# Attention on two double PSUM banks and feed-forward on four banks from step 8; shared blocks added into the PSUM bank in the last four chunks

## The chip, the core and the metric

The kernel runs on one core of a Trainium2 chip. Five engines work side by side, each through its own queue in program order: TensorE (PE) multiplies matrices and writes only PSUM; VectorE (DVE) and ScalarE (ACT) do elementwise work and read and write PSUM and SBUF; GpSimd (POOL) works on SBUF; SyncE (SP) issues most of the DMAs. They meet through semaphores. PSUM has eight banks; a bank holds 512 float32 numbers in each of 128 partitions. The metric is device time in microseconds; lower is better.

## The reference, cut to what matters

```
# attention, B,H,S,D = 4,8,768,48, per head and per time t
k_n = k / (|k| + 1e-6)
y[t] = q[t] @ state
state = state + beta[t] * outer(k_n[t], v[t] - state^T k_n[t])
# y goes to x of shape (B*S, H*D) = (3072, 384), then the feed-forward
h = x @ w_in                                        # w_in: 384 x 2048
g = maximum(h, 0) + alpha * minimum(h, 0)           # alpha: one slope per column of h
out = g @ w_out                                     # w_out: 2048 x 384
```

A recurrence over 768 positions, then a feed-forward of 3072 tokens with a PReLU between two matrix products. All is float32.

## The kernel before, in words

**Attention.** The 768 positions are cut into 12 chunks of 64. A chunk of all four batches is done in two *steps* (two batches each), so there are 24 steps n, and step n carries on the state of step n − 2. In each step the recurrence is solved with small matmuls: k times the state (`through_state`, L798), a triangular solve (`solve`, L823), the outputs (`outputs`, L836), the new state (`next_state`, L852), the query times the state (`query`, L783), grams of k for a step that comes nine later (`grams`, L500), small inverses (`between`, L732), and transposes of y into the feed-forward's input `xt` (`to_ffn`, L875). DVE inverts 32x32 blocks for four steps at a time (`eliminate`, L592 and L598). From step 8 on q, and from step 16 on k, are fetched as 32x32 blocks and turned by DVE (`turn_q`, L465; `turn_k`, L477). After its turn, every second `turn_k` has SP fetch the next chunk's keys; `load_q(n + 3)` fetches q for a later step.

**Feed-forward.** A chunk is 256 tokens. Chunks 2 to 7: `ffn_in` (L965) goes through eight *pairs* of 128 columns of h, each pair into one PSUM bank taken from `ps_ffn()`; ACT then writes Relu(−h) to SBUF (L975) and DVE makes g from it and from h in PSUM, one instruction for each half (the *slope*, L977). `ffn_out_fast` (L1030) multiplies by w_out with a scheme of seven instead of eight block products, each into a bank from `ps_ffn()`; DVE adds them up (L1050) and forms sums of operands ahead of them (L919). Chunks 8 to 11: `ffn_in_fast` uses the seven-product scheme for the input as well. A pair has six sub-steps. Two are for the *shared* products (L1198), which go into a bank of their own, from which ACT copies them to SBUF (`z`, L1217) and POOL adds them up (L1222). Four are for the pair's *own* products (L1188, L1193), in bank i mod 3. Then DVE adds z to the own bank and writes the sum h to SBUF (L1227, `total`), ACT takes Relu of it into another SBUF tile (L1232, `below`), and DVE makes g (L1236, `slope`). `ffn_out_faster` (L1282) is their output, L1278 its adds. A small list, `Due`, says after how many sub-steps (PER = 6 to a pair) each of the three is put into the program.

**PSUM.** Two banks, `ffn_banks[0:2]`, always belong to the feed-forward. `banks(pair, single)` shares out the other six: `big` is a rotating list of double banks (tiles `p_pair`) for attention, and further single banks (tiles `p_more`) are appended to `ffn_banks`. At first there are three doubles and no single; with step LATE = 16 there are two doubles and two singles. `ps_ffn()` flips between banks 0 and 1 in both cases; the two further banks are used only by chunks 8 to 11.

**The order of the work.** The order on each engine is the order in which the program puts the instructions, and that is written by hand. Each step n of the main loop has three bursts of attention, each followed by a *stretch* of feed-forward pieces from the generator `tail`: `burst_a(n)` (outputs and new state of step n − 1, k times the state, and the query while n < LATE), a stretch; `turn_round(n)` (transposes of step n − 1), a stretch; `burst_b(n)` (solve, grams, small inverses, and for n + 1 ≥ LATE the query of step n + 1), a stretch. `stretch` weaves its feed-forward pieces with a share of the block inversion and with the pieces that the burst returned as `later`; these are spread evenly from the fraction `soon` of the stretch on (0.5 unless given). A stretch has 8 to 18 pieces; `ffn_in` advances one matmul call at a time, an output product two. A matmul call appears in the profile as two records.

The turns are in `later` of `burst_a`, `load_q` is called straight from `turn_round`. The diff touches `ps_ffn` (L101), `through_state` (L801), `pair` in `ffn_in_fast` (L1172 to L1243), `burst_a` (L1383 to L1394), `burst_b` (L1403), `turn_round` (L1421 to L1423) and the main loop (from L1855 on).

Of the kernel before, what the change touches and what calls it, by code (L numbers as in the profile page):

```python
# [25 lines left out]
FP32 = mybir.dt.float32  # L26
# [6 lines left out]
C = 64  # L33
# [2 lines left out]
BUSY = 8  # L36
EARLY = 8
FIRST = 6
LATE = 16
FAST_IN = 8  # L40

# [2 lines left out]
def kernel(  # L44
# [53 lines left out]
    turn = [0]  # L98

    def ps_ffn():  # L100
        turn[0] ^= 1  # L101
        return ffn_banks[turn[0]]

    def half(i):
# [684 lines left out]
    def through_state(n, p=None, p_y=None):  # L789
        if n >= N:  # L790
            return []
        c, bp = steps[n]
        if c == 0:
            rhs_[n] = by_parity(nv[n])
            return []
        p = region(p, G * (D + C), g=G)
        for g, a, t in quarters():
            nc.tensor.matmul(  # L798
                p[half(t ^ a), a, g], k_t[n][dims(a), g, half(t)], beside[bp][dims(a), t, g]
            )  # L800
        asked = query(n, p_y) if n < LATE else []  # L801

        r = work.tile([128, 2, G, D], FP32, name="r")
        v_in = by_parity(nv[n])
        rhs_[n] = r

        def less(to, own, a):
            nc.vector.tensor_tensor(  # L808
                out=r[to, a], in0=v_in[to, a], in1=p[own, a, :, 0:D], op=ALU.subtract
            )  # L810

        return [
            lambda: less(slice(0, 128), slice(0, 128), 0),
            lambda: less(half(0), half(1), 1),
            lambda: less(half(1), half(0), 1),
            *asked,
            lambda: masked(n, p[:, :, :, D : D + C]),
        ]
# [333 lines left out]
    def ffn_in_fast(c):  # L1152
# [19 lines left out]
        def pair(i):  # L1172
            p = ffn_banks[i % 3]
            q = quarter(ffn_banks[2 if i == 0 else 3])
            z, g = terms(i), act_of(c, i)
            if "less" not in held:
                held["less"] = work.tile([128, G, 128], FP32, name="k_t", bufs=EARLY + 1)
            r = held["less"] if i % 2 == 0 else quarter(held["block"][:, 512:1024])
            r = r.rearrange("p (f u) e -> p f (u e)", f=2)

            def w(k, f):
                return w_in[:, k, (2 * i + f) * 128 : (2 * i + f + 1) * 128]
# [40 lines left out]
                yield  # L1223

            def total():
                h = g.rearrange("p f i -> p (f i)")
                nc.vector.tensor_tensor(  # L1227
                    out=h, in0=p, in1=z.rearrange("p i e -> p (i e)"), op=ALU.add
                )

            def below():
                nc.scalar.activation(r, g, ACT.Relu, scale=-1.0)  # L1232

            def slope():
                for f in range(2):
                    nc.vector.scalar_tensor_tensor(  # L1236
                        out=g[:, f], in0=r[:, f], scalar=al_t[:, 2 * i + f : 2 * i + f + 1],
                        in1=g[:, f], op0=ALU.mult, op1=ALU.add,
                    )

            due.put(PER * (i + 1) + {0: PER, FP - 1: 2}.get(i, 3), total)
            due.put(PER * (i + 2) + {FP - 2: 1, FP - 1: -4}.get(i, 2), below)
            due.put(PER * (i + 2) + {FP - 2: 1, FP - 1: -2}.get(i, 5), slope)  # L1243
            for gen in (own(), common()) if i == 0 else (common(), own()):
                for _ in gen:
                    due.step()
# [126 lines left out]
    def burst_a(n):  # L1373

        soon, later = [], []
        b = ps_big()
        if n > JOINED:
            soon += outputs(n - 1, b[:, :, 0:WY])
            soon += next_state(n - 1, b[:, :, WY : 2 * WY])
            later.append(lambda: load_late(n + 1))  # L1380
        if n < N:
            p = ps_big()
            y = ps_big()[:, :, 0:WY] if n < LATE else None  # L1383
            soon += through_state(n, p[:, :, 0 : G * (D + C)], y)
            if n < JOINED + 2:
                soon += between_1(n + 1, b[:, :, 2 * WY : 2 * WY + G * HB])
            if n == JOINED:
                soon += grams(n + EARLY, big[-1][:, :, WY : WY + G * C])
                later.append(lambda: squares(n + EARLY + 1))
            later.append(lambda: load_v(n + 3))  # L1390
            if TURNED_K <= n + EARLY + 1 < N:
                later.append(lambda: turn_k(n + EARLY + 1))
            if n + 2 < N:
                later.append(lambda: turn_q(n + 2))  # L1394
        now(soon)
        return later

    def burst_b(n):
# [1 line left out]
        b, x = ps_big(), ps_big()  # L1400
        soon = solve(n, b[:, :, 0:WY])
        gram = grams(n + EARLY + 1, x[:, :, 0 : G * C])
        asked = query(n + 1, x[:, :, 0:WY]) if n + 1 >= LATE else []  # L1403
        wanted = [(n + 1, True, b[:, :, WY : WY + G * HB])]
        if n > JOINED:
            wanted.append((n + 2, False, b[:, :, 2 * WY : 2 * WY + G * HB]))
# [7 lines left out]
    def turn_round(n):  # L1414

        if n > JOINED:
            to_ffn(n - 1)
        if n == JOINED:
            flips(n + EARLY + 1, N)
            load_keys(steps[TURNED_K][0])  # L1420
        later = weigh(n + EARLY + 1)  # L1421
        load_q(n + 3)
        return later  # L1423

    def each(pieces):
        for x in pieces:
# [426 lines left out]
    FILLS = [(12, 10, 12), (12, 18, 12)]  # L1853
    put_off = []
    for n in range(JOINED, N):  # L1855
        if n == LATE:
            banks(2, 2)
        fill, share = FILL.get(n, FILLS[n % 2]), PIECES_OF.get(n, TURNS[n % NJ])
        extra = [[], [], []]
# [10 lines left out]
        later = turn_round(n)  # L1870
        if n == JOINED:
            extra[1].append((placing(n + 1, (1, 2, 3)), PLACING))
        stretch(fill[1], blocks, share[1], later, *extra[1])
        m, ends = (n + 6) // NJ, n % NJ == 2
        if ends and n > JOINED:
            for _ in blocks:
# [55 lines left out]
```

## Time and profile before

| | us |
|---|---|
| median of three runs | 656.41 |
| range of the three | 654.98 to 656.82 |
| profiled execution, its own time | 656.53 |
| span of its trace | 654.8 |
| PE busy | 633.8 |
| DVE busy | 504.4 |
| ACT busy | 254.3 |
| POOL busy | 94.5 |

The span runs from the first to the last instruction; 1.7 us of the execution's time lie outside it. A row of the timeline gives start, duration, engine, line, operation, output and inputs, shape and how many were merged; a bracket at its end gives the idle time of the engine before it and what ended it. A row of groups gives, behind the bar, busy us and mean ns of one, then the idle time ahead of them and its releasers. A row of waits gives total us, how often, and the longest. PE's granted clock was 0.997 of full speed over the span.

### The profile page before, as it was taken

How to read it: one execution, taken by the hardware profiler on the slowest of the kernel's cores; microseconds unless marked ns; L12 is line 12 of the kernel's file. 1: busy time of each engine (PE TensorE's matmuls, PEld its weight loads, DVE VectorE, ACT ScalarE, POOL GpSimd, SP SyncE). 2: the span in 40 equal slices, each digit the busy share in tenths (PEclk: the TensorE clock that was granted, in tenths of full speed). 3: DMA queues.
4: the chain of work that ended last, by engine and by line, in shares of the span. 5: the costliest groups of instructions: out<-in, count | busy, mean ns of one | idle time of the engine just before them, and what ended most of it. 6: DMA issues, size and time to landing. Idle time of an engine off the chain costs nothing.

```text
span 654.8 us, 21590 instructions
## 1 busy us (share of the span) xinstructions
PE 633.8 (97%) x9199; PEld 558.2 (85%) x9199; DVE 504.4 (77%) x1206; ACT 254.3 (39%) x599; POOL 94.5 (14%) x204
## 2 busy tenths in 40 slices
PE   6989999999998998999998999999999999999997
PEld 4678888666777987988987988988989999999997
DVE  4976998967999789759969768868969659468383
ACT  5977565345443342243242242232135145042140
POOL 6001211010000000000000000000035044062260
PEclk9989999999999999999999999999999999999999
DMA  7956735212252241242242122122122210100000
GB/s 121 295 131 160 228 74 144 62 37 48 46 87 35 48 76 27 42 68 41 42 73 35 26 40 38 26 42 35 26 45 32 45 32 3 35 5 2 26 0 25
DMA packets 145968, 39.26 MB, mean 60 GB/s; under 512 B 139040, under 2 KB 142256, under 8 KB 145872
## 3 DMA queue, kind: packets, MB, share of 16 engines
q1 hardware_dynamic: 144000, 37.40, 28.0%
q8 instruction: 72, 1.18, 0.7%
q10 hardware_dynamic: 1872, 0.49, 0.4%
q14 instruction: 24, 0.20, 0.1%
HBM read 33.14 MB, written 4.72 MB: 58 GB/s over the span
## 4 chain that ended last, share of the span: by engine, by line
PE 76%; DVE 14%; ACT 3%; DMA 2%; issue 2%; SPq 1%; POOL 1%; DVEq 0%; POOLq 0%; ACTq 0%
PE p_ffn L1030 17%; PE p_ffn L965 13%; PE p_more L1282 8%; PE p_ffn L1008 5%; PE p_more L1198 5%; PE p_ffn L1188 3%; PE p_ffn L1282 3%; PE p_ffn L1193 2%; DVE act L977 2%; PE p_pair L732 2%; PE p_pair L823 2%; DVE block L598 2%; PE p_pair L1435 2%; DVE prod L592 2%; PE p_pair L677 2%
## 5 line engine op out<-in xcount | busy, mean ns | idle before, releaser
L965 PE MATMUL p_ffn<-xt,w_in 128*128 128x256 f32 x768 | 178.2, 385 | 7.8 <-DVE act L977 7.7
L965 PEld LDWEIGHTS p_ffn<-xt,w_in 128*128 128x128 f32 x768 | 142.9, 191 | 29.9 <-ACT act L975 5.0
L975 ACT ACTIVATE act<-p_ffn 128x512 f32<-128x512 f32 x56 | 33.3, 595 | 97.4 <-PE p_ffn L965 97.3
L977 DVE SCALAR_TENSOR_TENSOR act<-act,al_t,p_ffn 128x256 f32<-128x256 f32 x112 | 48.3, 472 | 25.7 <-ACT act L975 25.7
L598 DVE TENSOR_TENSOR block<-block,prod 128x30 f32<-128x30 f32 (+9 forms) x150 | 49.9, 332 | 5.2
L1222 POOL TENSOR_TENSOR k_t<-k_t 128x128 f32<-128x128 f32 (+1 forms) x48 | 29.4, 612 | 166.6 <-ACT k_t L1217 164.1
L1030 PE MATMUL p_ffn<-w_out,act 128*128 128x192 f32 x288 | 49.6, 329 | 0.7 <-ACT act L975 0.7
L592 DVE TENSOR_TENSOR prod<-block 128x30 f32<-128x30 f32 (+9 forms) x150 | 48.6, 324 | 1.5
L1030 PEld LDWEIGHTS p_ffn<-w_out,act 128*128 128x128 f32 x288 | 46.5, 190 | 1.3 <-ACT act L975 1.0
L417 POOL TENSOR_TENSOR beta_t<-beta_t,rec 128x8 f32<-128x8 f32 x24 | 6.2, 257 | 286.3 <-DVE rec L411 268.1
L877 ACT COPY xt<-p_pair 128x384 f32<-128x384 f32 x22 | 10.4, 478 | 92.3 <-PE p_pair L875 78.5
L1222 POOL TENSOR_TENSOR block<-block 128x128 f32<-128x128 f32 (+1 forms) x48 | 27.6, 576 | 16.0 <-ACT block L1217 13.5
L1188 PE MATMUL p_ffn<-xt,w_in 128*128 128x256 f32 x96 | 28.8, 381 | 0.5 <-DVE o_sb L1050 0.5
L808 DVE TENSOR_TENSOR r<-v_raw,p_pair 64x192 f32<-64x192 f32 (+1 forms) x66 | 23.3, 352 | 2.3 <-PE p_pair L798 1.2
L827 DVE TENSOR_TENSOR u<-p_pair,wgt 128x384 f32<-128x384 f32 x24 | 13.2, 555 | 14.6 <-PE p_pair L732 14.0
L744 ACT COPY inv<-p_pair 32x256 f32<-32x256 f32 x40 | 14.4, 361 | 25.7 <-DVE u L827 24.9
L1236 DVE SCALAR_TENSOR_TENSOR act<-block,al_t,act 128x256 f32<-128x256 f32 x32 | 19.7, 657 | 3.6 <-ACT block L1232 3.4
L1008 PE MATMUL p_ffn<-w_out,act 128*128 128x384 f32 x64 | 21.8, 491 | 0.3 <-DVE more L977 0.3
L1282 PE MATMUL p_more<-w_out,act 128*128 128x192 f32 x128 | 21.9, 329 | 0.0
L1217 ACT COPY k_t<-p_more 128x512 f32<-128x512 f32 x16 | 9.4, 585 | 31.6 <-PE p_more L1198 29.3
L798 PE MATMUL p_pair<-beside,k_t 48*64 48x112 f32 x704 | 21.4, 259 | 0.2 <-ACT beside L456 0.2
L787 ACT COPY y<-p_pair 128x384 f32<-128x384 f32 x22 | 10.4, 477 | 28.5 <-PE p_pair L783 26.9
(232 smaller groups left out, 1382.0 us busy)
## 6 DMA issues: line engine op xcount, KB each, us to landing
w_out<-in_moe_w_in_dram SPq DMA_DIRECT2D x10, 512.0 KB, 5.2
v_raw<-in_v_dram SPq DMA_DIRECT2D x48, 96.0 KB, 2.9
kl<-in_k_dram SPq DMA_DIRECT2D x96, 48.0 KB, 2.5
out_dram<-o_sb SPq DMA_DIRECT2D x90, 48.0 KB, 1.7
space_out<-in_moe_w_out_dram SPq DMA_DIRECT2D x11, 384.0 KB, 4.2
ke_last<-in_k_dram SPq DMA_DIRECT2D x25, 96.0 KB, 2.8
qp<-in_q_dram SPq DMA_DIRECT2D x64, 32.0 KB, 2.3
w_out<-in_moe_w_out_dram SPq DMA_DIRECT2D x5, 384.0 KB, 3.5
```

Of the source, the lines that this page charges most:

```text
L592: nc.vector.tensor_tensor(out=prod, in0=r[:, 0:j, j : j + 1].to_broadcast([128, j, n]), in1=r[:, j : j + 1, j + 1 : HB].to_broadcast([128, ...
L598: nc.vector.tensor_tensor(out=r[:, 0:j, j + 1 : HB], in0=r[:, 0:j, j + 1 : HB], in1=prod, op=ALU.add)
L808: nc.vector.tensor_tensor(out=r[to, a], in0=v_in[to, a], in1=p[own, a, :, 0:D], op=ALU.subtract)
L965: nc.tensor.matmul(p_h[:, i], w_in[:, t, (f + i) * 128 : (f + i + 1) * 128], xt[:, t], start=(t == 0), stop=(t == KT - 1),)
L975: nc.scalar.activation(g, p_h, ACT.Relu, scale=-1.0)
L977: nc.vector.scalar_tensor_tensor(out=g[:, i], in0=g[:, i], scalar=al_t[:, f + i : f + i + 1], in1=p_h[:, i], op0=ALU.mult, op1=ALU.add,)
L1008: nc.tensor.matmul(p_o[u], gs[f // 2][:, f % 2, u * 128 : (u + 1) * 128], w_out[:, f], start=(f == 0), stop=(f == FT - 1),)
L1030: nc.tensor.matmul(p, x(i), w(i), start=(i == 0), stop=(i == FP - 1))
L1188: nc.tensor.matmul(p[:, f * 256 : f * 256 + 256], w(2, f), xt[:, 2], start=True, stop=False)
L1198: nc.tensor.matmul(q[:, j], a, b, start=True, stop=True)
L1222: nc.gpsimd.tensor_tensor(out=dst, in0=a, in1=b, op=ALU.add)
L1282: nc.tensor.matmul(p, x(i), w(i), start=(i == 0), stop=(i == FP - 1))
```

## The change

It does four things.

1. `banks(2, 2)` is called at step NARROW = 8 instead of step 16, and `ps_ffn()` goes round all banks of `ffn_banks`, so from step 8 on it takes four in turn.
2. From step 8 on the query of step n + 1 is in `burst_b(n)`, in the second half of the gram's bank, instead of in a double of its own in `burst_a`.
3. `turn_k`, `turn_q` and `load_q` go into `later` of `turn_round`, ahead of and behind the weights of k, and its stretch begins to place them at 0.2.
4. In chunks 8 to 11, `total` writes the sum back to the PSUM bank; Relu reads it there and writes g's place; the slope reads Relu's result in SBUF and the sum in PSUM. Relu is due at 6(i + 1) + 4 instead of 6(i + 2) + 2, the slope at 6(i + 2) + 1 instead of 6(i + 2) + 5, with other counts for the first and the last two pairs. The tile that held Relu's result is no longer there.

```diff
+NARROW = 8
 LATE = 16
...
     def ps_ffn():
-        turn[0] ^= 1
+        turn[0] = (turn[0] + 1) % len(ffn_banks)
         return ffn_banks[turn[0]]
...
-        asked = query(n, p_y) if n < LATE else []
+        asked = query(n, p_y) if n < NARROW else []
...
-            if "less" not in held:
-                held["less"] = work.tile([128, G, 128], FP32, name="k_t", bufs=EARLY + 1)
-            r = held["less"] if i % 2 == 0 else quarter(held["block"][:, 512:1024])
-            r = r.rearrange("p (f u) e -> p f (u e)", f=2)
...
             def total():
-                h = g.rearrange("p f i -> p (f i)")
                 nc.vector.tensor_tensor(
-                    out=h, in0=p, in1=z.rearrange("p i e -> p (i e)"), op=ALU.add
+                    out=p, in0=p, in1=z.rearrange("p i e -> p (i e)"), op=ALU.add
                 )
 
             def below():
-                nc.scalar.activation(r, g, ACT.Relu, scale=-1.0)
+                nc.scalar.activation(g, p.rearrange("p (f i) -> p f i", f=2), ACT.Relu, scale=-1.0)
 
             def slope():
                 for f in range(2):
                     nc.vector.scalar_tensor_tensor(
-                        out=g[:, f], in0=r[:, f], scalar=al_t[:, 2 * i + f : 2 * i + f + 1],
-                        in1=g[:, f], op0=ALU.mult, op1=ALU.add,
+                        out=g[:, f], in0=g[:, f], scalar=al_t[:, 2 * i + f : 2 * i + f + 1],
+                        in1=p[:, f * 256 : f * 256 + 256], op0=ALU.mult, op1=ALU.add,
                     )
 
             due.put(PER * (i + 1) + {0: PER, FP - 1: 2}.get(i, 3), total)
-            due.put(PER * (i + 2) + {FP - 2: 1, FP - 1: -4}.get(i, 2), below)
-            due.put(PER * (i + 2) + {FP - 2: 1, FP - 1: -2}.get(i, 5), slope)
+            due.put(PER * (i + 1) + {0: PER + 1, FP - 1: 2}.get(i, 4), below)
+            due.put(PER * (i + 2) + {0: 3, FP - 2: 1, FP - 1: -2}.get(i, 1), slope)
...
-            y = ps_big()[:, :, 0:WY] if n < LATE else None
+            y = ps_big()[:, :, 0:WY] if n < NARROW else None
...
             later.append(lambda: load_v(n + 3))
-            if TURNED_K <= n + EARLY + 1 < N:
-                later.append(lambda: turn_k(n + EARLY + 1))
-            if n + 2 < N:
-                later.append(lambda: turn_q(n + 2))
...
-        asked = query(n + 1, x[:, :, 0:WY]) if n + 1 >= LATE else []
+        asked = query(n + 1, x[:, :, G * C : G * C + WY]) if n + 1 >= NARROW else []
...
-        later = weigh(n + EARLY + 1)
-        load_q(n + 3)
-        return later
+        later = []
+        if TURNED_K <= n + EARLY + 1 < N:
+            later.append(lambda: turn_k(n + EARLY + 1))
+        if n + 2 < N:
+            later.append(lambda: turn_q(n + 2))
+        later += weigh(n + EARLY + 1)
+        return later + [lambda: load_q(n + 3)]
...
-        if n == LATE:
+        if n == NARROW:
             banks(2, 2)
...
-        stretch(fill[1], blocks, share[1], later, *extra[1])
+        stretch(fill[1], blocks, share[1], later, *extra[1], soon=0.2)
```

## The prediction

> **What bounds the kernel now.** The page comes first: its busy times, then the costliest group. TensorE (PE) is busy almost everywhere, so time can only come from the few places where it stands still, or from the last store.
>
> ```profile
> span 654.8 us, 21590 instructions
> PE 633.8 (97%) x9199; PEld 558.2 (85%) x9199; DVE 504.4 (77%) x1206; ACT 254.3 (39%) x599; POOL 94.5 (14%) x204
> L965 PE MATMUL p_ffn<-xt,w_in 128*128 128x256 f32 x768 | 178.2, 385 | 7.8 <-DVE act L977 7.7
> ```
>
> PE is idle for 654.8 − 633.8 = 21.0 us. The banks change with step 8, whose first burst is this:
>
> ```profile
> 218.56 0.68 PE L836 MATMUL p_pair<-u,a_t 64*64 64x48 f32 x32
> ```
>
> So I ask for PE's waits from 215 us to the end; the answer has two lines, and asked from 480 us on it has none:
>
> ```profile
> PE p_ffn L965 <- DVE act L977: 5.9, 6, 1.5
> PE p_ffn L1188 <- DVE o_sb L1050: 0.5, 1, 0.5
> ```
>
> Both are waits for a feed-forward bank. With two banks, the matmuls of pair i of a chunk need the bank of pair i − 2, which is free only when VectorE (DVE) has run both slope instructions of that pair (L977). The PE timeline shows where each wait stands (the bracket is the idle time before the row):
>
> ```profile
> 246.43 0.49 PE L875 MATMUL p_pair<-ident,y 128*128 128x128 f32 x3
> 248.46 2.83 PE L965 MATMUL p_ffn<-xt,w_in 128*128 128x256 f32 x12 [1.54 <-DVE act L977]
> 252.53 1.32 PE L965 MATMUL p_ffn<-xt,w_in 128*128 128x256 f32 x5 [1.24 <-DVE act L977]
> ...
> 298.01 0.49 PE L875 MATMUL p_pair<-ident,y 128*128 128x128 f32 x3
> 299.24 0.46 PE L965 MATMUL p_ffn<-xt,w_in 128*128 128x256 f32 x1 [0.74 <-DVE act L977]
> ...
> 347.48 0.49 PE L875 MATMUL p_pair<-ident,y 128*128 128x128 f32 x3
> 348.57 2.83 PE L965 MATMUL p_ffn<-xt,w_in 128*128 128x256 f32 x12 [0.60 <-DVE act L977]
> 352.63 0.67 PE L965 MATMUL p_ffn<-xt,w_in 128*128 128x256 f32 x2 [1.24 <-DVE act L977]
> ...
> 425.73 0.49 PE L875 MATMUL p_pair<-ident,y 128*128 128x128 f32 x3
> 426.06 0.49 PE L1030 MATMUL p_ffn<-w_out,act 128*128 128x192 f32 x2
> ...
> 445.52 0.49 PE L875 MATMUL p_pair<-ident,y 128*128 128x128 f32 x3
> 446.04 2.83 PE L965 MATMUL p_ffn<-xt,w_in 128*128 128x256 f32 x12
> 449.45 0.89 PE L965 MATMUL p_ffn<-xt,w_in 128*128 128x256 f32 x3 [0.58 <-DVE act L977]
> ...
> 477.85 0.67 PE L1188 MATMUL p_ffn<-xt,w_in 128*128 128x256 f32 x2 [0.54 <-DVE o_sb L1050]
> ```
>
> All lie in odd steps (9, 11, 13, 17), just after the transposes of L875, while DVE still works off the attention burst, and at the start of chunk 8. One correction is needed. Twelve matmuls fill 2.83 us, so one starts every 0.22 us, but one record lasts 0.39 us (the 385 above): a matmul record runs on 0.17 us after the next could have started, and a gap inside a row of matmuls shows 0.17 us too little. After L875 the undisturbed distance is 426.06 − 425.73 = 0.33 us.
>
> **The change part by part.**
>
> *Four feed-forward banks.* Pair i now takes the bank of pair i − 4. A pair is 12 records, 12 × 0.22 = 2.6 us, so PE may run 5.2 us further ahead of DVE than before, and the longest wait was 1.5 us. Each wait is valued by starts. After L875: 248.46 − 246.43 − 0.33 = 1.70; 299.24 − 298.01 − 0.33 = 0.90; 348.57 − 347.48 − 0.33 = 0.76; 446.04 − 445.52 − 0.33 = 0.19. Inside L965: 1.24 + 0.17 = 1.41, twice, and 0.58 + 0.17 = 0.75. Together 7.1 us.
>
> The wait of L1188 is the start of chunk 8: its pair 0 uses bank 0, and the last product of chunk 7's output stands there too. Rotating over four from the switch (in the fifth of the seven products of chunk 2's output, each chunk taking 8 + 7 turns), that last product lands in bank 2. Pair 0 uses bank 2 only after its own four pieces, some 1.5 us later. The wait goes, 0.54 + 0.16 = 0.7 us. **Sum of what goes: 7.8 us.** PE is what ends the rest of the kernel, without a wait from 480 us on, so I count it in full.
>
> *What is late next.* PE runs ahead of DVE, so DVE could be late at the next thing PE needs: the last pair's slopes, which the first output product reads in its last eighth. In step 9 the timeline has:
>
> ```profile
> 249.51 0.76 DVE L477 STREAM_TRANSPOSE k_t<-ke_pair 128x256 f32<-128x256 f32 x2
> ...
> 250.91 0.71 DVE L465 STREAM_TRANSPOSE beside<-qp 128x512 f32<-128x512 f32 x1
> 251.55 0.83 DVE L977 SCALAR_TENSOR_TENSOR act<-act,al_t,p_ffn 128x256 f32<-128x256 f32 x2
> ...
> 256.02 0.87 DVE L977 SCALAR_TENSOR_TENSOR act<-act,al_t,p_ffn 128x256 f32<-128x256 f32 x2 [0.40 <-ACT act L975]
> ...
> 258.61 0.87 DVE L977 SCALAR_TENSOR_TENSOR act<-act,al_t,p_ffn 128x256 f32<-128x256 f32 x2 [0.58 <-ACT act L975]
> ...
> 259.65 4.66 PE L1030 MATMUL p_ffn<-w_out,act 128*128 128x192 f32 x27
> ```
>
> DVE's last slopes ended at 258.61 + 0.87 = 259.48. Ahead of them DVE idled 0.40 + 0.58 us, for Relu results that PE had delivered late; without PE's waits they end at 258.5. The output (L1030) would start 1.70 + 1.41 = 3.1 us earlier, at 256.55, and need them after seven of its eight operands, 14 records of 4.66 / 27 = 0.17 us, at 258.9. It fits, by 0.4 us. Step 13 has the same order, with 2.2 us of waits to go and so 0.9 us more room. I take nothing here; if DVE did not gain its 1 us, the wait would be 0.6 us in step 9.
>
> *Two doubles for attention.* The bursts of steps 8 to 15 rotate over two double banks instead of three. Each burst then finds the bank that the burst before it left, whose readers (L827, L506, L744, L787) follow that burst at once, a whole stretch of feed-forward ahead. Steps 16 on run this way already, and the list of waits has no line for L836, L798, L823 or L783 there. Nothing. If that cover went, a burst would wait for the last copy of the one before.
>
> *The query's 16 matmuls* move from the first burst into the second, in steps 8 to 15, with their ACT copy (L787): the same instructions, and the state that they read was updated a half step before. Nothing on PE.
>
> *The turns.* L477 (0.76 us) and L465 (0.71 us) move from the first stretch of each step to the second, at 20% and 40% of it, and the q fetch goes to its end. In odd steps the slopes that PE waited for come ahead of them, the same stall again, so this adds no term. What waits for them: the grams of the second burst read the turned k. In step 9 that burst ends where L1030 starts, at 256.55 by the sum above, and the last turn had run by 250.91 + 0.71 = 251.6 even behind the backlog. On SP, the eight key fetches of an even step wait for the turn and stand ahead of the q fetch and the stores; all are needed a step later. Nothing; each us by which a turn came after its grams would be a us of PE.
>
> *The last four chunks* (from 477 us). The sum of own and shared products is added back into the PSUM bank, Relu and slope read it there, so a bank is free after the slope, not after the sum. DVE rows:
>
> ```profile
> L1227 DVE TENSOR_TENSOR act<-p_ffn,block 128x512 f32<-128x512 f32 x12 | 8.2, 685 | 8.2 <-ACT y L787 4.4 <-POOL block L1222 3.8
> L1236 DVE SCALAR_TENSOR_TENSOR act<-k_t,al_t,act 128x256 f32<-128x256 f32 x32 | 20.5, 680 | 0.1
> L975 ACT ACTIVATE act<-p_ffn 128x512 f32<-128x512 f32 x56 | 33.3, 595 | 97.4 <-PE p_ffn L965 97.3
> L977 DVE SCALAR_TENSOR_TENSOR act<-act,al_t,p_ffn 128x256 f32<-128x256 f32 x112 | 48.3, 472 | 25.7 <-ACT act L975 25.7
> ```
>
> The new slope is L977's form (one operand in PSUM): 472 ns against 680, so DVE saves some 0.2 us in each of 64, work that PE does not wait for. A DVE instruction that writes PSUM stands in no row. Upward I bound the sum by two L1236 of half its width, 1.36 us; downward by the 0.2 us that a PSUM operand saves there, 0.48. I take the nearest row, L1227: the same operation, width and inputs, 0.69. At 1.36 the copy of the shared bank, which comes behind sum and Relu, would be 0.7 us late in chunks 8, 9 and 10: 2 us more. At 0.48 nothing changes.
>
> [...]
>
> Now the bank. Slope of pair i is due one sub-step into pair i + 2, and pair i + 3 writes the same bank in its third: seven sub-steps. Before, eleven lay between. The attention burst falls into this just ahead of pair 3:
>
> ```profile
> 491.54 0.69 DVE L520 TENSOR_TENSOR a_t<-p_pair,minus 128x512 f32<-128x512 f32 x1
> 492.15 0.68 DVE L1227 TENSOR_TENSOR act<-p_more,k_t 128x512 f32<-128x512 f32 x1
> 492.49 0.60 PE L1188 MATMUL p_ffn<-xt,w_in 128*128 128x256 f32 x2
> ...
> 537.61 0.69 DVE L520 TENSOR_TENSOR a_t<-p_pair,minus 128x512 f32<-128x512 f32 x1
> 538.22 0.68 DVE L1227 TENSOR_TENSOR act<-p_more,k_t 128x512 f32<-128x512 f32 x1
> 538.58 0.60 PE L1188 MATMUL p_ffn<-xt,w_in 128*128 128x256 f32 x2
> ...
> 581.82 0.60 PE L1188 MATMUL p_ffn<-xt,w_in 128*128 128x256 f32 x2
> ...
> 583.08 0.68 DVE L1227 TENSOR_TENSOR act<-p_more,k_t 128x512 f32<-128x512 f32 x1
> ...
> 584.24 0.60 PE L1188 MATMUL p_ffn<-xt,w_in 128*128 128x256 f32 x2
> ```
>
> Pair 3 and pair 4 write their banks at 581.82 and 584.24, so a sub-step lasts 2.42 / 6 = 0.40 us. By the new counts pair 1's slope takes the place behind L520 where L1227 stands now, 0.83 us by the row at 251.55, and PE starts 0.15 us after it (252.53 against 251.55 + 0.83). In chunk 8 bank 1 is free at 492.15 + 0.83 + 0.15 = 493.13, and pair 4 wants it at 492.49: **0.64 us**. In chunk 9: 539.20 − 538.58 = **0.62 us**. In chunk 10 (a shorter burst) 584.06 against 584.24: none. Chunk 11 has no attention beside it. New waits: 1.3 us. Queued behind the waiting matmul is all of PE, so they count in full. ACT's Relu, four sub-steps earlier, now stands ahead of the copy that frees the shared bank (L1217) and waits for the late sum; that copy ends about when the delayed PE comes for it, so I add nothing.
>
> **Sum:** 656.53 (the profiled execution) − 7.8 + 1.3 = **650.0 us**. That execution is 0.1 us over the median of the three, 656.41, so the sum stands for the median as well.
>
> **The rivals.** *No new wait* (the matmul needs only half the bank, or DVE comes sooner): 656.5 − 7.8 = 648.7. Against it: at 252.53 PE had waited for both slopes, though it writes the first half first. *DVE's debt moves on:* the waits of steps 9 and 13 return at the output product or at the burst, half of their 5.3 us, and the shared bank's copy costs 0.3 us twice: 650.0 + 2.6 + 0.6 = 653.2. For it speaks the 0.4 us of room in step 9; against it, that DVE is idle again in the outputs. *The banks don't matter:* if DVE's rate and not its order made the waits, all would return, 656. Against: DVE is 77% busy. *Slower:* the sum, Relu and slope on one bank become the bound of chunks 8 to 11. Undisturbed they take 0.68 + 0.60 + 0.83 and three hand-overs of 0.15, 2.6 us, from a sum to a bank wanted eleven sub-steps, 4.4 us, after it: 1.8 us of room. If the sum into PSUM took over 2.5 us instead of 0.68, each of some 30 reuses would wait; at 2.9 us that is 0.4 × 30 = 12 us, 656.5 − 7.8 + 12 = 661. No row is near that.
>
> **How the numbers follow.** Forecast 650.0 with its neighbourhood (649.2 to 651.5) 0.55; no new wait 0.15; debt moves on 0.16; banks don't matter 0.08; slower 0.06. The range runs from 648.0 (the first rival, and 0.7 us for smaller bubbles) to 653.5 (the second). About 0.3% (2 us) is what a measurement of this kernel can tell from no change: faster 0.86, same 0.08, slower 0.06.
>
> **What would show it.** In the profile after: no wait of the input matmuls (L965 before) for slopes after 218 us; no wait at the start of chunk 8; two waits of about 0.6 us of the chunk 8 and 9 matmuls for a slope, at pair 4; slopes of the last chunks near 475 ns; the sum near 0.69 us. Wrong would be a wait of the first output product or of a burst on DVE, a sum over 1 us, or waits in most pairs of chunks 8 to 11.

## The result and the profile after

The changed kernel takes 649.0 us (median of four runs, 647.67 to 650.18) where the one before, measured beside it, takes 656.57 (654.98 to 656.82). The ratio is 0.989, with a 95% interval of 0.986 to 0.992: faster by 1.1%, 7.6 us. The forecast was 650.0.

The page of the profile after, an execution of 647.67 us. In groups, the columns are busy us and mean ns of one, then the idle time ahead of them:

```profile
span 645.9 us, 21572 instructions
PE 630.5 (98%) x9199; PEld 555.8 (86%) x9199; DVE 491.6 (76%) x1206; ACT 252.7 (39%) x599; POOL 91.4 (14%) x204
L966 PE MATMUL p_ffn<-xt,w_in 128*128 128x256 f32 x528 | 123.1, 384 | 1.8 <-DVE act L978 1.8
L1232 DVE SCALAR_TENSOR_TENSOR act<-act,al_t,p_ffn 128x256 f32<-128x256 f32 x48 | 20.9, 476 | 15.5 <-ACT act L1228 15.3
L507 DVE TENSOR_TENSOR same<-p_pair,wgt 128x256 f32<-128x256 f32 x24 | 10.1, 422 | 21.2 <-ACT y L788 17.0
```

The input matmuls waited 7.7 us for slopes before; now 1.8, in steps 6 and 7, ahead of the switch. The slopes of the last chunks take 476 ns instead of 657 to 680. The wait in the last line is new: DVE stands idle for 17.0 us ahead of its weighted copies of the grams (L507), behind ACT's copy of the query (L788). Before, the same line was:

```profile
L506 DVE TENSOR_TENSOR same<-p_pair,wgt 128x256 f32<-128x256 f32 x24 | 10.0, 418 | 4.1 <-POOL same L549 1.6 <-PE p_pair L500 1.5 <-POOL wgt L418 0.9
```

PE's waits from 215 us to the end were two lines before. After:

```profile
PE p_more L1031 <- DVE sums L920: 0.4, 1, 0.4
```

It is a new wait, and no slope stands in it. That list has nothing under about 0.2 us of shown idle time, so I measure by starts instead. The first matmul of "k times the state" opens each step's first burst. In the timeline it is, for step 6, in the kernel before and in the one after:

```profile
173.22 0.52 PE L798 MATMUL p_pair<-beside,k_t 48*64 48x112 f32 x12 [0.18 <-ACT beside L456]
```

```profile
171.79 0.52 PE L799 MATMUL p_pair<-beside,k_t 48*64 48x112 f32 x12 [0.19 <-ACT beside L457]
```

From there to the end of the span are 654.82 − 173.22 = 481.6 us and 645.95 − 171.79 = 474.16: 7.43 us gained. The other 1.43 us between the two spans lie ahead of step 6. In the kernels below that point moves between 170.72 and 174.09 from one execution to the next, so I leave it out. This table gives the distance from each step's first burst to the next one's, where it differs by over 0.1 us, and the total from step 6 on:

| kernel | 7 | 9 | 11 | 13 | 15 | 17 | 18 | 19 | 21 | 23 to end | total |
|---|---|---|---|---|---|---|---|---|---|---|---|
| before | 25.21 | 28.70 | 26.60 | 27.77 | 25.44 | 26.08 | 22.75 | 24.17 | 24.17 | 74.89 | 481.59 |
| after | 25.14 | 26.13 | 25.46 | 25.46 | 24.99 | 24.99 | 21.98 | 24.75 | 24.73 | 74.80 | 474.16 |
| banks only | 25.71 | 25.79 | 25.46 | 25.46 | 24.99 | 24.99 | 21.98 | 24.17 | 24.17 | 74.88 | 473.43 |
| turns only | 24.53 | 28.06 | 26.44 | 26.41 | 25.46 | 25.38 | 22.85 | 24.17 | 24.17 | 74.87 | 478.05 |
| in place only | 25.28 | 28.71 | 26.57 | 27.77 | 25.44 | 26.08 | 22.76 | 24.74 | 24.73 | 74.78 | 482.68 |
| three banks | 25.13 | 26.12 | 25.46 | 25.46 | 24.99 | 24.99 | 22.84 | 24.74 | 24.72 | 74.80 | 474.99 |
| gram first | 24.92 | 25.46 | 25.46 | 25.46 | 24.99 | 24.99 | 21.98 | 24.74 | 24.73 | 74.80 | 473.24 |
| not in place | 25.11 | 26.11 | 25.46 | 25.46 | 24.99 | 24.99 | 21.98 | 24.17 | 24.17 | 74.88 | 473.04 |
| slope ahead | 25.14 | 26.12 | 25.46 | 25.46 | 24.99 | 24.99 | 21.98 | 24.56 | 24.63 | 74.79 | 473.83 |
| Relu behind | 25.13 | 26.13 | 25.46 | 25.46 | 24.99 | 24.99 | 21.98 | 25.46 | 26.11 | 77.41 | 478.85 |
| best | 24.98 | 25.46 | 25.46 | 25.46 | 24.99 | 24.99 | 21.98 | 24.17 | 24.17 | 74.87 | 472.26 |
| from 7, by two | 24.87 | 25.46 | 25.46 | 25.46 | 24.99 | 24.99 | 21.98 | 24.17 | 24.17 | 74.89 | 472.54 |
| from 7, by one | 26.43 | 25.46 | 25.46 | 25.46 | 24.99 | 24.99 | 21.98 | 24.17 | 24.17 | 74.88 | 474.09 |
| after, again | 25.18 | 26.13 | 25.46 | 25.46 | 24.99 | 24.99 | 21.98 | 24.75 | 24.73 | 74.80 | 474.19 |

The last row is a second measurement of the changed kernel; its total is 0.03 us from the first. (Steps 7 and 15 hold a query more and a query less where the query is moved, 0.45 us each way; with the switch at step 7 the query moves into step 6, which is 0.4 us longer and not in the table.)

### The profile page after: what moved, and what is told of

It reads as the page before. It is cut to its first block, busy times and chain, and to the rows that moved or that the text cites. A ratio compares the mean times of both kernels' runs of the same rounds, so it can differ in the third digit from the quotient of the medians.

```text
span 645.9 us, 21572 instructions
## 1 busy us (share of the span) xinstructions
PE 630.5 (98%) x9199; PEld 555.8 (86%) x9199; DVE 491.6 (76%) x1206; ACT 252.7 (39%) x599; POOL 91.4 (14%) x204
## 4 chain that ended last, share of the span: by engine, by line
PE 74%; DVE 14%; DMA 5%; ACT 2%; SPq 2%; issue 1%; ACTq 0%; DVEq 0%
PE p_ffn L966 11%; PE p_more L1278 8%; PE p_more L1031 7%; PE p_ffn L1031 7%; PE p_more L966 7%; PE p_ffn L1009 5%; PE p_more L1195 4%; PE p_ffn L1278 3%; PE p_ffn L1185 3%; DMA ke_pair<-in_k_dram 2%; PE p_ffn L1190 2%; PE p_pair L799 2%; DVE block L599 2%; DVE prod L593 2%; PE p_pair L837 2%; PE p_pair L824 2%
## 5 line engine op out<-in xcount | busy, mean ns | idle before, releaser
L966 PE MATMUL p_ffn<-xt,w_in 128*128 128x256 f32 x528 | 123.1, 384 | 1.8 <-DVE act L978 1.8
L966 PEld LDWEIGHTS p_ffn<-xt,w_in 128*128 128x128 f32 x528 | 97.4, 190 | 16.0 <-ACT wgt L718 1.6
L966 PE MATMUL p_more<-xt,w_in 128*128 128x256 f32 x240 | 54.8, 381 | 0.0
L1219 POOL TENSOR_TENSOR k_t<-k_t 128x128 f32<-128x128 f32 (+1 forms) x48 | 28.7, 598 | 168.5 <-ACT k_t L1214 161.9
L966 PEld LDWEIGHTS p_more<-xt,w_in 128*128 128x128 f32 x240 | 45.0, 190 | 6.3
L976 ACT ACTIVATE act<-p_ffn 128x512 f32<-128x512 f32 x36 | 21.4, 594 | 51.0 <-PE p_ffn L966 50.9
L978 DVE SCALAR_TENSOR_TENSOR act<-act,al_t,p_ffn 128x256 f32<-128x256 f32 x72 | 30.9, 470 | 8.0 <-ACT act L976 8.0
L1232 DVE SCALAR_TENSOR_TENSOR act<-act,al_t,p_ffn 128x256 f32<-128x256 f32 x48 | 20.9, 476 | 15.5 <-ACT act L1228 15.3
L1185 PE MATMUL p_ffn<-xt,w_in 128*128 128x256 f32 x96 | 28.9, 382 | 0.1
L1219 POOL TENSOR_TENSOR block<-block 128x128 f32<-128x128 f32 (+1 forms) x48 | 26.2, 546 | 14.7 <-ACT block L1214 12.2
L1031 PE MATMUL p_ffn<-w_out,act 128*128 128x192 f32 x160 | 27.9, 330 | 0.0
L745 ACT COPY inv<-p_pair 32x256 f32<-32x256 f32 x40 | 14.5, 362 | 33.1 <-DVE u L828 32.3
L976 ACT ACTIVATE act<-p_more 128x512 f32<-128x512 f32 x20 | 11.9, 595 | 37.2 <-PE p_more L966 37.2
L507 DVE TENSOR_TENSOR same<-p_pair,wgt 128x256 f32<-128x256 f32 x24 | 10.1, 422 | 21.2 <-ACT y L788 17.0
L1031 PEld LDWEIGHTS p_ffn<-w_out,act 128*128 128x128 f32 x160 | 25.9, 190 | 0.4
L1228 ACT ACTIVATE act<-p_ffn 128x512 f32<-128x512 f32 x24 | 14.3, 598 | 23.5 <-DVE p_ffn L1223 23.4
```

The source lines that it names most:

```text
L966: nc.tensor.matmul(p_h[:, i], w_in[:, t, (f + i) * 128 : (f + i + 1) * 128], xt[:, t], start=(t == 0), stop=(t == KT - 1),)
L976: nc.scalar.activation(g, p_h, ACT.Relu, scale=-1.0)
L978: nc.vector.scalar_tensor_tensor(out=g[:, i], in0=g[:, i], scalar=al_t[:, f + i : f + i + 1], in1=p_h[:, i], op0=ALU.mult, op1=ALU.add,)
L1031: nc.tensor.matmul(p, x(i), w(i), start=(i == 0), stop=(i == FP - 1))
L1185: nc.tensor.matmul(p[:, f * 256 : f * 256 + 256], w(2, f), xt[:, 2], start=True, stop=False)
L1219: nc.gpsimd.tensor_tensor(out=dst, in0=a, in1=b, op=ALU.add)
```

## The experiments

All of them compute the whole of the reference. The theory is the prediction's: the banks make the gain, and the in-place sum gives back about 1.3 us. The rivals: the turns, moved behind the slopes, make the gain; or the cheaper slopes do; or the changed order of the query matters.

**Banks and query alone** (parts 1 and 2; turns and last chunks as before).

```diff
+NARROW = 8
-        turn[0] ^= 1
+        turn[0] = (turn[0] + 1) % len(ffn_banks)
-        asked = query(n, p_y) if n < LATE else []
+        asked = query(n, p_y) if n < NARROW else []
...
-        if n == LATE:
+        if n == NARROW:
             banks(2, 2)
```

> The kernel before with the banks and the query of the change alone (parts 1 and 2): turns in the first stretch, sum in SBUF in the last four chunks. Measured from the first matmul of step 6's first burst to the end of the span: 481.6 us before, 474.2 us after the change. Theory (the feed-forward bank made the waits): the waits of L965 in steps 9, 11, 13 and 17 and the one at the start of chunk 8 go, the wait for the operand sums in step 9 stays, and there is no wait at pair 4 of chunks 8 and 9: 473.5 to 474.5. Rival (the moved turns are what brought the slopes forward): most of the waits stay, 477 or more.

Measured: 648.49 us (647.02 to 649.08), ratio 0.987 [0.984, 0.990]; 473.43 by starts. Two of the change's four parts give all of its gain, and 0.73 us more. PE's waits from 170 us on, but for one of 0.2 us at the first burst of step 6, which stands in the kernels before and after too:

```profile
PE p_ffn L966 <- DVE act L978: 1.8, 2, 1.4
PE p_ffn L1031 <- ACT act L976: 0.7, 1, 0.7
```

The first line is steps 6 and 7, ahead of the switch. The second is step 7, as in the kernel before: the first output product waits there for Relu and slope of the last pair. The change as a whole no longer has it. No run moves the query without the banks, but the kernel before tells the two apart: its step 17 already has the query in the second burst and two doubles, still with two feed-forward banks in turn, and it waits for slopes (0.58 us shown); with four banks that step goes from 26.08 to 24.99.

**Turns alone** (part 3; two banks).

```diff
-            if TURNED_K <= n + EARLY + 1 < N:
-                later.append(lambda: turn_k(n + EARLY + 1))
-            if n + 2 < N:
-                later.append(lambda: turn_q(n + 2))
...
+        later += weigh(n + EARLY + 1)
+        return later + [lambda: load_q(n + 3)]
...
+        stretch(fill[1], blocks, share[1], later, *extra[1], soon=0.2)
```

> The kernel before with the moved turns alone (part 3), two feed-forward banks as before. Theory: the bank waits that stand behind the turns in DVE's order go (the second waits of steps 9 and 13, 1.4 us each, the one of step 17, 0.75, and one of 0.7 in step 7), the others stay (1.70, 0.90 and 0.76 after L875, and 0.7 at the start of chunk 8): from step 6's first burst to the end about 477, against 481.6 before. Rival (only banks count): 481 or more. Rival (the turns bring all): 475 or less.

Measured: 652.13 us (651.67 to 652.38), ratio 0.993 [0.990, 0.995]; 478.05, 3.54 us gained. Steps 7, 13 and 17 gain 0.68, 1.36 and 0.70 as expected, step 9 only 0.64. Its two waits now stand so:

```profile
242.97 2.83 PE L965 MATMUL p_ffn<-xt,w_in 128*128 128x256 f32 x12 [0.35 <-DVE act L977]
...
247.79 8.12 PE L965 MATMUL p_ffn<-xt,w_in 128*128 128x256 f32 x36 [1.66 <-DVE act L977]
```

The second wait of before is gone, the first stands, and a small one has come ahead of it, in the first stretch. The turns now stand in step 8's second stretch, and DVE comes out of it later: its slopes ahead of the small wait start only 0.68 us earlier than before (241.96 against 242.64), where PE begins step 9 1.39 us earlier (238.42 against 239.81). 3.5 us by the turns and 8.2 us by the banks don't add up to the 7.4 of the whole: they cure the same waits, and with four banks the turns have nothing left to cure but step 7.

**In place alone** (part 4).

```diff
-                    out=h, in0=p, in1=z.rearrange("p i e -> p (i e)"), op=ALU.add
+                    out=p, in0=p, in1=z.rearrange("p i e -> p (i e)"), op=ALU.add
-            due.put(PER * (i + 2) + {FP - 2: 1, FP - 1: -4}.get(i, 2), below)
-            due.put(PER * (i + 2) + {FP - 2: 1, FP - 1: -2}.get(i, 5), slope)
+            due.put(PER * (i + 1) + {0: PER + 1, FP - 1: 2}.get(i, 4), below)
+            due.put(PER * (i + 2) + {0: 3, FP - 2: 1, FP - 1: -2}.get(i, 1), slope)
```

> The kernel before with the last four chunks of the change alone (part 4). Theory: two waits of about 0.6 us, at pair 4 and 5 of chunks 8 and 9, and nothing gained: 482.7 from step 6's first burst to the end, against 481.6. Rival (the cheaper slopes on DVE pay): 481.6 or less.

Measured: 657.46 us (655.12 to 658.72), ratio 1.001 [0.999, 1.003], too near to tell in the time; by starts 482.68, and the whole loss stands in steps 19 and 21, 0.57 and 0.56 us. Chunks 8 to 11 get nothing from 64 cheaper slopes.

**The change without part 4.**

```diff
-                    out=p, in0=p, in1=z.rearrange("p i e -> p (i e)"), op=ALU.add
+                    out=h, in0=p, in1=z.rearrange("p i e -> p (i e)"), op=ALU.add
...
-            due.put(PER * (i + 2) + {0: 3, FP - 2: 1, FP - 1: -2}.get(i, 1), slope)
+            due.put(PER * (i + 2) + {FP - 2: 1, FP - 1: -2}.get(i, 5), slope)
```

> The changed kernel without the change of the last four chunks (sum, Relu and slope as before). Theory (in place costs two waits of 0.58 us and gains nothing): 473.0 from step 6's first burst to the end, against 474.2. Rival (cheaper slopes pay somewhere, in the outputs or at the end): 474.2 or more.

Measured: 647.64 us (646.99 to 648.85), ratio 0.986 [0.983, 0.989]; 473.04. The 1.1 us of steps 19 and 21 come back, from either side the same number.

**Three banks instead of four.**

```diff
-        turn[0] = (turn[0] + 1) % len(ffn_banks)
+        turn[0] = (turn[0] + 1) % min(3, len(ffn_banks))
```

> The changed kernel, but the feed-forward of chunks 2 to 7 goes round three banks of its four. Theory: PE then may run 2.6 us ahead of DVE, still more than the longest wait of before (1.5 us), so no L965 wait comes back; with three in turn the last product of chunk 7 falls on bank 0 again and the wait of 0.7 us at the start of chunk 8 returns: 474.9 from step 6's first burst to the end, against 474.2 with four. Rival (four are needed): L965 waits return and it is 476 or more.

Measured: 648.83 us (648.4 to 650.55), ratio 0.988 [0.985, 0.991]; 474.99. Steps 9 to 17 are those of four banks within 0.02 us. The one wait from 215 us on is the start of chunk 8:

```profile
PE p_ffn L1185 <- DVE o_sb L1051: 0.6, 1, 0.6
```

One bank more than before would do for the slopes. The fourth pays only through the count of turns: with three, the last product of chunk 7's output again falls on bank 0, and step 18 is 0.86 us longer.

**Gram ahead of the query in the second burst.** In the kernel after, the wait for `sums` is in step 9. Rows of its timeline:

```profile
256.39 0.87 DVE L978 SCALAR_TENSOR_TENSOR act<-act,al_t,p_more 128x256 f32<-128x256 f32 x2
257.18 0.55 DVE L828 TENSOR_TENSOR u<-p_pair,wgt 128x384 f32<-128x384 f32 x1
257.76 0.74 ACT L745 COPY inv<-p_pair 32x256 f32<-32x256 f32 x2 [4.47 <-DVE u L828]
258.51 0.74 ACT L745 COPY mid<-p_pair 32x256 f32<-32x256 f32 x2
259.28 0.48 ACT L788 COPY y<-p_pair 128x384 f32<-128x384 f32 x1
...
259.86 0.42 DVE L507 TENSOR_TENSOR same<-p_pair,wgt 128x256 f32<-128x256 f32 x1 [2.13 <-ACT y L788]
...
261.25 0.69 DVE L920 TENSOR_TENSOR sums<-sums,act 128x512 f32<-128x512 f32 x1
...
261.99 1.57 PE L1031 MATMUL p_more<-more,sums 128*128 128x192 f32 x8 [0.41 <-DVE sums L920]
```

The query's product now lies in the gram's bank. ACT copies it out (L788), behind four copies of small inverses (L745), and that copy stands ahead of DVE's reads of the gram (L507) in the program; they follow it, though they read other columns. DVE stands still for 2.13 us and comes late with the sums that the next product reads. So:

```diff
-        now(soon + asked + gram[:2])
+        now(soon + gram[:2] + asked)
```

> The changed kernel with one line's order turned round: in the second burst of steps 7 to 14 DVE's two weighted copies of the gram are put ahead of ACT's copy of the query, which lies in the same bank. Theory (after the change DVE idles about 2 us per step for ACT's query copy, which stands ahead of it in that bank, and that makes the sums late on which PE waits in step 9): DVE's idle time before the weighted copies falls from 17 us to 3 or less and step 9's wait of 0.67 us goes: 473.5 us from step 6's first burst to the end, against 474.2 with the change. Rival (DVE simply has too much work in step 9): 474.1 or more.

Measured: 647.32 us (646.74 to 648.72), ratio 0.986 [0.983, 0.989]; 473.24. Step 9 loses its last wait (26.13 to 25.46), step 7 gains 0.22. Its timeline:

```profile
257.32 0.55 DVE L828 TENSOR_TENSOR u<-p_pair,wgt 128x384 f32<-128x384 f32 x1
257.79 0.42 DVE L507 TENSOR_TENSOR same<-p_pair,wgt 128x256 f32<-128x256 f32 x1
...
258.45 0.68 DVE L920 TENSOR_TENSOR sums<-act 128x512 f32<-128x512 f32 x1
```

DVE goes on without a pause. Its 17.0 us of idle time were worth 0.9 us; the rest had cover.

**The slope of pair 1 one sub-step earlier.** The wait of chunk 8, in the kernel after:

```profile
481.27 0.69 DVE L521 TENSOR_TENSOR a_t<-p_pair,minus 128x512 f32<-128x512 f32 x1
481.88 0.86 DVE L1232 SCALAR_TENSOR_TENSOR act<-act,al_t,p_ffn 128x256 f32<-128x256 f32 x2
482.35 0.39 PE L1195 MATMUL p_more<-k_t,same 128*128 128x128 f32 x2
482.66 0.69 DVE L1223 TENSOR_TENSOR p_more<-p_more,k_t 128x512 f32<-128x512 f32 x1
482.80 0.30 PEld L1185 LDWEIGHTS p_ffn<-xt,w_in 128*128 128x128 f32 x2 [0.25 <-DVE act L1232]
482.80 0.70 PE L1185 MATMUL p_ffn<-xt,w_in 128*128 128x256 f32 x2
...
483.34 0.61 PE L1190 MATMUL p_ffn<-xt,w_in 128*128 128x128 f32 x4
483.39 0.60 ACT L1228 ACTIVATE act<-p_more 128x512 f32<-128x512 f32 x1 [2.38 <-DVE p_more L1223]
484.28 0.58 ACT L1214 COPY k_t<-p_more 128x512 f32<-128x512 f32 x1
484.44 0.49 PE L876 MATMUL p_pair<-ident,y 128*128 128x128 f32 x3
484.91 0.30 PEld L1195 LDWEIGHTS p_more<-xt,w_in 128*128 128x128 f32 x2 [0.23 <-ACT k_t L1214]
484.92 0.49 PE L1195 MATMUL p_more<-xt,w_in 128*128 128x128 f32 x2
```

There are two waits: PE at 482.80 for the slopes that end at 482.74, and at 484.91 for the copy of the shared bank that ends at 484.86, late because Relu waited ahead of it for the sum.

```diff
-            due.put(PER * (i + 2) + {0: 3, FP - 2: 1, FP - 1: -2}.get(i, 1), slope)
+            due.put(PER * (i + 2) + {0: 3, 1: 0, FP - 2: 1, FP - 1: -2}.get(i, 1), slope)
```

> The changed kernel with pair 1's slope in the last four chunks put ahead of the attention burst on DVE, so that bank 1 is free in good time. Theory (two waits share the 0.58 us: 0.33 for the bank at pair 4, 0.25 for the copy of the shared bank, which stands behind a Relu that waits for a late sum): the first wait goes and the second grows by nearly as much, 473.8 to 474.2. Rival (the bank alone): both go, 473.0.

Measured: 648.89 us (647.66 to 651.16), ratio 0.988 [0.985, 0.992]; 473.83. The bank's wait is gone. The copy's stays, and steps 19 and 21 are still 0.39 and 0.46 us over 24.17. PE's waits from 215 us on have the step 9 line and this:

```profile
PE p_more L1195 <- ACT k_t L1214: 0.2, 1, 0.2
```

**Relu behind the copy again** (Relu four sub-steps later, slope two).

```diff
-            due.put(PER * (i + 1) + {0: PER + 1, FP - 1: 2}.get(i, 4), below)
-            due.put(PER * (i + 2) + {0: 3, FP - 2: 1, FP - 1: -2}.get(i, 1), slope)
+            due.put(PER * (i + 2) + {FP - 2: 1, FP - 1: -4}.get(i, 2), below)
+            due.put(PER * (i + 2) + {FP - 2: 1, FP - 1: -2}.get(i, 3), slope)
```

> The changed kernel with Relu of the last four chunks due after the copy of the shared bank again, as before the change, and the slope two sub-steps later; still all in the PSUM bank. DVE's order is the same. Theory (two waits): the copy's wait of 0.25 us goes, the bank's of 0.33 stays, in chunks 8 and 9: 473.7 from step 6's first burst to the end, against 474.2. Rival (the bank alone, PE then waits less for nothing else): 474.2.

Measured: 652.61 us (651.84 to 653.18), ratio 0.993 [0.991, 0.996]; 478.85, five us over the expectation. Rows of its timeline, chunk 8:

```profile
485.09 0.49 PE L876 MATMUL p_pair<-ident,y 128*128 128x128 f32 x3
...
485.41 0.39 PE L1195 MATMUL p_more<-xt,w_in 128*128 128x128 f32 x2
...
486.76 0.59 ACT L1214 COPY block<-p_more 128x512 f32<-128x512 f32 x1 [0.67 <-DVE p_ffn L1223]
487.25 0.60 ACT L1228 ACTIVATE act<-p_ffn 128x512 f32<-128x512 f32 x1
487.88 0.87 DVE L1232 SCALAR_TENSOR_TENSOR act<-act,al_t,p_ffn 128x256 f32<-128x256 f32 x2 [1.23 <-ACT act L1228]
488.51 0.39 PE L1195 MATMUL p_more<-k_t,same 128*128 128x128 f32 x2
...
488.90 0.46 PE L1185 MATMUL p_ffn<-xt,w_in 128*128 128x256 f32 x1
```

The copy's wait did go (485.41 − 485.09 = 0.32 us, the undisturbed distance; 0.48 in the kernel after). But the slope of a pair with no attention beside it now ends at 487.88 + 0.87 = 488.75, and the matmul that wants its bank starts at 488.90, 0.39 instead of 0.22 us behind the one before. Ten such pairs, two each in chunks 8 to 10 and four in chunk 11, lose 0.24 to 0.29 us each against the kernel after, counted by starts; that is 2.7 of the 4.7 us between the two totals. I had left the quiet pairs out of the count. Most of the rest is in three other places. The wait at pair 4 of chunks 8 and 9 did not stay but grew, from 0.5 us shown for the two to 1.1, and the output of chunk 11 waits for a slope too, worth 0.8 us by starts:

```profile
PE p_ffn L1185 <- DVE act L1232: 1.1, 2, 0.6
PE p_more L1278 <- DVE act L1232: 0.5, 1, 0.5
```

In step 21 the small inverses (L733) come 0.6 us late; the profile names no releaser there.

**Gram first, and not in place**: the two edits that gained, together.

> The changed kernel without the change of the last four chunks and with DVE's gram copies ahead of ACT's query copy: the two runs that gained, together. Theory (they act in different stages and add up): 474.2 - 1.1 - 0.9 = 472.1 us from step 6's first burst to the end, no wait of PE left behind step 7, time about 2 us under the changed kernel's. Rival (one gain eats the other): 473.0.

Measured: 646.79 us (646.55 to 647.78), ratio 0.986 [0.984, 0.988]; 472.26, the sum of both gains to 0.2 us. On the same chip the changed kernel again took 648.42 us (646.66 to 649.87; ratio 0.988 [0.986, 0.989]), for which this was expected:

> The changed kernel once more, beside the two above on the same chip: 474.2 from step 6's first burst to the end, and a time about 2 us over the first of them.

The medians differ by 1.6 us, the totals by 1.93. By starts it is the best version found.

**The same from step 7 on**, to get rid of the 1.4 us that are left there; the turn is set on at the switch by two, so that chunk 7's last product again ends in bank 2, or by one, so that the last two pairs of chunk 2's input take the two new banks.

```diff
+NARROW = 7
...
             banks(2, 2)
+            turn[0] += 2
```

> The same, with the two doubles and four feed-forward banks from step 7 instead of 8 (and the rotation started two banks on, so that chunk 7's last product again ends in bank 2). Theory (the last large bank wait, 1.35 us shown in step 7 with two banks, is of the same kind): it goes, with its 0.17 and a restart of 0.08: 470.5 from step 6's first burst to the end. Rival (in step 7 DVE itself is too late): the wait moves to the first output product, 471.5 to 472.

Measured: 646.25 us (645.55 to 651.83), ratio 0.986 [0.983, 0.989]; 472.54. By the times it cannot be told from the best version; by starts it gains nothing, since the wait stays:

```profile
201.96 2.83 PE L966 MATMUL p_ffn<-xt,w_in 128*128 128x256 f32 x12 [1.79 <-DVE act L978]
```

With the turn two on, the last pair of chunk 2 takes the bank of the pair two before it: the same wait for the same slope. With `turn[0] += 1`:

> As the run from step 7, but the rotation starts one bank on instead of two, so that the last two pairs of chunk 2's input take the two banks that step 7 adds; in that run the last pair took the bank of the pair two before it, as with two banks. Theory (the rotation kept the wait alive): step 7's wait goes, and from step 6's first burst to the end it takes 470.6 to 471.0 us, against 472.3 with the switch at step 8. Rival (DVE itself is too late in step 7): the wait stays or moves to the first output product, 471.8 or more.

Measured: 647.14 us (646.38 to 648.87), ratio 0.986 [0.984, 0.988]; 474.09. The pair no longer waits; the first output product does, at its last operand:

```profile
203.31 2.44 PE L1031 MATMUL p_ffn<-w_out,act 128*128 128x192 f32 x14
...
204.71 0.69 DVE L920 TENSOR_TENSOR sums<-act,sums 128x512 f32<-128x512 f32 x1
205.31 0.76 DVE L478 STREAM_TRANSPOSE k_t<-ke_pair 128x256 f32<-128x256 f32 x2
...
206.52 0.67 DVE L466 STREAM_TRANSPOSE beside<-qp 128x512 f32<-128x512 f32 x1
207.11 0.83 DVE L978 SCALAR_TENSOR_TENSOR act<-act,al_t,p_more 128x256 f32<-128x256 f32 x2
207.60 2.68 PE L1031 MATMUL p_ffn<-w_out,act 128*128 128x192 f32 x10 [1.85 <-DVE act L978]
```

The last pair's slopes come behind 2.4 us of sums and transposes (204.71 to 207.11). Here DVE's debt moves on, as the rival said; PE gained nothing from its earlier start: the matmul behind the wait comes 207.60 − 194.45 = 13.15 us after step 7's first burst, the same one in the best version 206.79 − 193.59 = 13.20. Step 7 is still 1.45 us longer than in the best version; all of that lies behind this point, and its reason is told at the end.

## Why the prediction was right, point by point

**The banks make the gain: shown.** Banks and query alone bring 8.2 us, turns alone 3.5, in place alone −1.1. The waits of steps 11, 13, 17 and 18, forecast at 0.90, 2.17, 0.94 and 0.70, gave 1.14, 2.31, 1.09 and 0.77; step 9 gives 3.24 once its new wait is off, against 3.11. Together 8.55 for 7.8: each wait cost some 0.1 us more than its start distance, because the first matmul after a wait is followed late too. The rows of the kernel after show such a start: from 482.80 to 483.34 are 0.54 us for two records, 0.44 undisturbed.

**The step that failed: "*The query's 16 matmuls* move ... Nothing on PE."** The matmuls cost nothing. But the copy that empties them came to stand ahead of DVE's reads of the same bank: DVE lost 2.1 us a step, and 0.67 us of it reached PE in step 9. I had followed the instructions that move, and not what they share a bank with. "DVE's debt" was rightly named as the risk; the product asked about, the first, was in time (its slopes end at 257.26, and the list of waits has no line for it); the late one was the next, with `sums`.

**Two doubles for attention, nothing: held.** No burst waits for a double in the list of waits. **The turns, no term: nearly.** They took away step 7's wait at the output product: 25.71 to 25.14 from banks alone to the whole. In step 9 they took back 0.34 (25.79 to 26.13).

**The new waits in chunks 8 and 9: sum right, split wrong.** Forecast 0.64 and 0.62, measured 0.58 and 0.56, none in chunk 10. But the bank has only about 0.33 us of it: DVE's L521 came 0.35 us sooner than forecast, counted back from the matmul that waits (482.35 + 0.22 − 481.27 = 1.30 us, against 492.49 − 491.54 = 0.95), and the hand-over took 0.06 us (482.74 to 482.80), not 0.15. The other 0.25 is the copy of the shared bank, to which I had given nothing because the delayed PE would come just then. PE's matmul, wanted 0.33 us behind the row at 484.44, came 0.15 us late. The experiment with the slope ahead separates the two.

**The sum into PSUM: right.** 691 to 700 ns, taken as 0.69 from the neighbour that writes SBUF. From the groups by tile, after:

```profile
L1223 DVE TENSOR_TENSOR p_ffn<-p_ffn,k_t x12: 692/699/700, 473.1 to 623.3; 128x512 f32<-128x512 f32 x12
L1232 DVE SCALAR_TENSOR_TENSOR act<-act,al_t,p_ffn x48: 470/476/482, 476.2 to 627.2; 128x256 f32<-128x256 f32 x48
```

and before (least, median, longest ns):

```profile
L1236 DVE SCALAR_TENSOR_TENSOR act<-k_t,al_t,act x32: 469/674/949, 487.3 to 634.8; 128x256 f32<-128x256 f32 x32
```

The shortest slope takes 469 ns in both forms. What goes away is the spread above it, not a fixed price; the 0.2 us that the prediction took for the gain of a PSUM operand (680 against 472) is the mean of that spread. GpSimd's adds (L1222 before, L1219 after) work beside these slopes, and slope by slope the two traces show: before, the 20 of the 64 slopes that no GpSimd instruction overlaps take 469 to 486 ns, and the 37 that one overlaps for over 0.5 us take 585 to 950; after, 39 of 64 are overlapped, 11 of them from end to end, and none takes more than 482. That GpSimd makes the long ones fits these numbers, but no kernel took its work away, so no edit tested it.

**The slower rival: did not come, but is near.** Its mechanism is what Relu behind the copy ran into. There the 1.8 us of room are used up by moving Relu four sub-steps (1.6 us) and putting it behind a copy, and the quiet pairs start to pay. I had tied it to a sum of over 2.5 us; the place of Relu is what decides it.

**From 650.0 to the result.** From step 6 on: forecast −7.8 + 1.3 = −6.5, measured −7.43. Of the difference, about 0.75 is larger bubbles, 0.1 smaller new waits, 0.5 the turns in step 7 (25.21 + 0.45 − 25.14), and −0.67 the query's copy; steps 6 and 23 bring 0.2. That the total came within 1 us is in part luck, since these misses have both signs.

## What to carry to other kernels

In this kernel a wait for a buffer was cured by one more buffer or by moving what stood ahead of the release, and not twice: 8.16 us with the banks and the query, 3.54 with the turns, 8.55 with both. When a tile is moved into a shared bank, look at who reads the bank's other half and which read comes first in the program: the reader that someone waits for goes first. Here the other order cost DVE 17.0 us of idle time and the kernel 0.9 us. And look whether the engine behind a wait is itself late: in step 7, with the switch one step earlier, the freed buffer only moved the wait to the next thing that DVE makes, from 1.79 us at the last pair (by two) to 1.85 at the output product (by one).

## What the runs showed of the hardware that was not expected

In the last kernel (from 7, by one), PE's pause ahead of 207.60 was followed by a stretch at half clock. Its windows (PE, PEld, DVE, ACT and POOL busy us, then the granted clock, DMA share and GB/s):

```profile
205.14:208.55 3.41, 1.56 (x10) 1.27 (x9) 3.41 (x9) 0.32 (x1) 0.00 (x0) 1.00 0.24 29
208.55:211.96 3.41, 3.41 (x70) 2.97 (x72) 3.38 (x7) 0.00 (x0) 0.41 (x2) 0.50 0.00 0
211.96:215.37 3.41, 3.41 (x121) 3.31 (x114) 1.93 (x6) 1.42 (x4) 1.42 (x2) 1.00 0.02 5
```

The half-clock stretch lasts 3.41 us. The matmul of the wait came level with the best version's (13.15 against 13.20 us into step 7), and the first matmul of the query behind it 1.45 us late (211.97 − 194.45 = 17.52 against 209.66 − 193.59 = 16.07), so the half clock cost 1.5 us; without it this kernel's total would be about 472.6, an estimate from the two, and about level with the best. Ahead of it PE stood still for 1.85 us. After waits of 1.66 (turns alone) and 1.79 us (from 7, by two) the granted clock stayed at 1.00. In the kernel before, a pause of 1.27 us ahead of 45.05 was followed by half clock, again for 3.41 us (45.28 to 48.69), and one of 1.54 us ahead of 248.46 was not. PE's busy share of the 3.41 us ahead doesn't decide it alone: it was 46% ahead of the half clock here and 60% in the kernel before (41.86 to 45.28), but in the same kernel 55% (245.70 to 249.11) was not followed by half clock. What decides stays open.
